# Decay attention with a softplus FFN on one core: operand moves on GpSimd's DMA queue, and a rearranged first batch

## The chip, the core and the metric

The kernel runs on one core of a Trainium2 chip. The metric is device time in microseconds (us); lower is better. A core has TensorE (PE in the profile, with its weight loads as PEld), VectorE (DVE), ScalarE (ACT), GpSimd (POOL) and SyncE (SP), which here only issues DMAs. Each engine has one instruction stream that it works through in order; the DMAs that an engine issues form its queue.

## What is computed

Two stages, in float32, one after the other on the same tokens. Batch 8, 8 heads, 576 positions, head size 64; the FFN has 512 inputs and outputs and 2048 hidden units.

```python
scores = scale * np.matmul(q, k.transpose(0, 1, 3, 2))       # scale = 1/8
cum = np.cumsum(np.log(np.clip(f, 0.0001, 1.0)), axis=-1)
decay = cum[:, :, :, None] - cum[:, :, None, :]
scores = np.where(causal, -1000000000.0, scores + decay)
attn = softmax(scores)                                       # over the last axis
x = (attn @ v), heads side by side: [4608, 512]
h = x @ w_in
g = np.maximum(h, 0.0) + np.log1p(np.exp(-np.abs(h)))
out = g @ w_out
```

The weights arrive as float64 and are turned into float32 on the chip (`load_f64`, line 422: a scaling and a sign part on ACT, a clip, a low part and a join).

## The kernel before

**The planner.** Nothing is emitted directly. Each piece of work is added to a list with a modelled cost on one engine (or on several to choose from), the pieces it comes after, and the buffers it takes (`Plan.add`, line 66). `Plan.run` (line 105) then simulates all engines and emits the piece that can start first, earlier-added pieces first among equals, until none is left. So modelled costs (`on_pe32`, `on_turn`, `on_dma`, from line 157) and due times set the order in which every engine's instructions stand in its stream. What the chip really takes shows only in the trace. Where the plan sees a gap on PE of over 0.5 us before the FFN's first accumulation, `fill_gap` (line 1487) puts small matmuls on a constant mask there (L1492), and three more such matmuls stand at the start (`warm`, L1481).

**The first batch ("plain").** Batch 0 is worked on in plain float32 matmuls, in 14 jobs: two quads (`first`, line 563: four heads, tokens 0 to 128), four pairs (`second`, line 573: two heads, tokens 128 to 256) and eight rests (`rest`, line 584: one head, tokens 256 to 576). The scores (L787) take q and k with two further rows, so that 66 rows are multiplied: the rows are the running sums `cum` and a constant of 8, in crossed order, and their products add the decay terms to the scores. They come by DMA: q and k from `in_qkT` (L687 for quads and pairs, L671 for rests), the two rows from the tile `cum` (L691, L674), each row by a DMA of its own. `cum` is made by a clip (L360), a logarithm (L363) and a scan in two steps: columns 0 to 256 (L376), then the rest (L381). Row minima (L794, on DVE), the exponential (L814, on ACT), transposes of the weights ("turn", L895), matmuls that spread the reciprocals (L899), and the product with v (L968, `output_tiled`) follow. In `output_tiled` the matmuls are grouped in one step for each bank of transposed weights. Meanwhile the weights are loaded (L440) in pieces of 512 KB; the FFN for tokens 0 to 256 is also plain (L1158 up, L1281 down).

**All other batches ("whole", line 552).** 56 jobs, one for each head of batches 1 to 7. Operands are split into a high and a low part, so that a product takes several faster matmuls. `prepare` (line 730) makes the tile `T` of a head: the high part of q and k by a cast (`hi`, L742), the low part by a subtraction (`lo`, L745), and four moves of 144 KB each from one half of the partitions to the other (L748), named k3, q1, k2 and q0 in the code. k3 comes after `hi`, q1 after `lo`, k2 after q1, and q0 after all of them, so that q1, k2 and q0 are three DMAs in a row. All four are issued by SP. The scores of the head (L789, L790) wait for q0. The weights of a head are scaled by the reciprocal sums before the turn (`scale`, line 839: on ACT L842, on DVE or POOL L844, as the plan chooses).

**Around them.** SP's queue also carries the loads of the next heads (L710 for q and k, L652 and L656 for v), the FFN's low weights (L1150, 512 KB each), its kept activations (L1236, L1317) and the output (L1359). The main loop (line 1496) adds, for each job in turn, its scores, turns and products, the `prepare` of the next job and the loads of the one after, some weight loads (`W_EACH`, line 1524: three for each job, two for each of the first six), and a share of the FFN's work that has come due.

Of the kernel before, what the change touches and what calls it, by code (L numbers as in the profile page):

```python
# [11 lines left out]
F32 = mybir.dt.float32  # L12
# [12 lines left out]
SCALE_BIAS = 1.0  # L25
# [25 lines left out]
class Plan:  # L51
# [53 lines left out]
    def run(self, engines):  # L105
        clock = dict.fromkeys(engines, 0.0)
        done, base, n = [False] * len(self.ops), 0, len(self.ops)
        while base < n:
            best = None
            for op in self.ops[base : base + WINDOW]:  # L110
                if done[op.at] or op.missing:
                    continue
                s = self.start_of(op, clock)
                if s and (best is None or (s[0], op.rank) < best[0]):
                    best = (s[0], op.rank), op, s
            _, op, (op.start, on) = best
# [42 lines left out]
    return On("PE", times * (max(n * 0.000444, m * 0.00092) + 0.002))  # L159


def on_pe32(n):

    return On("PE", 4 * n / 2400 + 0.004)


def on_turn(n):

    return On("PE", 0.109 * n)
# [49 lines left out]
def tile_decay_attention_softplus_ffn(  # L219
# [128 lines left out]


    decay_ready, cum_used, first_rows, cum = {}, [], [], {}  # L350

    def decay():
        box = {}
# [15 lines left out]
        def eights(e, t, value):  # L369
            e.memset(cum["x"][:, t, :], value)  # L370

        def scan(e):

            c = cum[0]
            x = box["f"][:, 0:256]
            e.tensor_tensor_scan(c[:, 0:256], x, x, 0.0, ALU.add, ALU.min)  # L376

        def scan_rest(e):
            c = cum[0]
            x = box["f"][:, 256:S]  # L380
            e.tensor_tensor_scan(c[:, 256:S], x, x, c[:, 255:256], ALU.add, ALU.min)  # L381

        def split(e):
            ch, cl = box["hl"] = [buf("raw", [P, S], f"c{x}", F32R)[0:BH] for x in "hl"]
# [37 lines left out]
    def load_f64(src, new, name, takes=()):  # L422
# [29 lines left out]
        def low(e):  # L452
            box["x"] = new()
            out = halves_of(box["x"], 2)[:, :, 0]
            x = halves_of(box["s"].rearrange("p c t -> p (c t)"), 4)[:, :, 1]
            scale, bias = 2.0**-13, 2.0**-14 - 0.5
            if e is nc.scalar:
                e.activation(out, x, AF.Copy, scale=scale, bias=bias)
            else:
                e.tensor_scalar(out, x, scale, bias, ALU.mult, ALU.add)  # L460

        def sign(e):
            out = halves_of(box["x"], 2)[:, :, 1].bitcast(F16)
# [8 lines left out]
        on = [On("POOL", 1.95), on_dve(512, True, bias=SCALE_BIAS)]  # L472
        cl = add(on, clip, after=[sc])
        lw = add(On("POOL", 1.95), low, after=[ld], takes=takes)
# [128 lines left out]
    def attention(job):  # L603
# [65 lines left out]
        def load32():  # L669
            def qk(e):  # L670
                e.dma_start(out=qk32[0:64], in_=qkT[b, :, heads[0]])  # L671

            def rows(e, x):
                e.dma_start(out=qk32[64 + x : 65 + x], in_=cum["x"][bh : bh + 1, 1 - x : 3 - x])  # L674
# [7 lines left out]
            cum_used.append(add(NO_ENGINE, mark, after=y))  # L682
            st["T"] = [x] + y

        def load_quad():
            def qk(e, h):
# [43 lines left out]
        def prepare():  # L730
# [26 lines left out]
            h_ = add(copies(S), hi, after=[start, st["qk"]])  # L757
            l_ = add(On("DVE", 0.75, 0.0, True), lo, after=[h_])
            give("raw", [l_])
            k3 = add_dma(move(low, 3, top, 0), 144, after=[h_])  # L760
            q1 = add_dma(move(low, 1, low, 2), 144, after=[l_])
            k2 = add_dma(move(low, 2, top, 0), 144, after=[q1])
            q0_ = add_dma(move(top, 0, low, 0), 144, after=[k2, k3, l_])
            st["T"] = [a, q0_]


        def stat_tile(ti):
# [12 lines left out]
            for i, (a, z, acc) in enumerate(pieces):  # L780
# [1 line left out]
                final = z == end  # L782

                def scores(e, box=box, a=a, z=z):
                    o = box["o"] = bank("att", f"s{n}_{ti}_{a}")[0:n_q, 0 : z - a]
                    if plain:
                        e.matmul(o, part32(0, q0, end), part32(1, a, z), start=True, stop=True)  # L787
                        return
                    e.matmul(o, qA[:, q0:end], kA[:, a:z], start=True, stop=False)  # L789
                    e.matmul(o, qB[0:ST, q0:end], kB[0:ST, a:z], start=False, stop=True)  # L790

                def row_min(e, box=box, w=z - a, i=i, final=final):
# [8 lines left out]
                o = add(on, scores, after=st["T"], takes=("att",), loose=True)  # L801
                m = add(
                    On("DVE", 0.076 + (z - a) / 960), row_min, lag=0.2, after=[o] + mask_set + stat_set,
                    takes=("stat",) if ti == 0 and i == 0 else (),
# [49 lines left out]
        def weights(bi):  # L854
# [69 lines left out]
            m = add(on_turn(len(blocks) - 0.48 * small + 2 * len(sums)), turn, after=need, takes=("att",))  # L924
# [18 lines left out]
        def output_tiled():  # L943

            steps = [[] for _ in banks]
            for gi, (g0, g1, r, c0) in enumerate(groups):
                todo = [x for x in parts if x[0] < g1 and x[1] > g0]
                todo.sort(key=lambda x: (max(x[0], g0) > g0, x[2]))
                for lo, hi, bi, vc, at, pbox, ready, _ in todo:
                    a, z = max(lo, g0), min(hi, g1)  # L950
                    mm = dict(
                        g=gi, r=64 * r, a=a - g0 + c0, z=z - g0 + c0, vc=vc, p=pbox, o=at + a - lo,
                        ready=ready,
                    )
                    steps[bi].append(mm)
                mms = [m for ms in steps for m in ms if m["g"] == gi]
                for m in mms:
                    m.update(start=m is mms[0], stop=m is mms[-1])
            box, before = {}, []
            for i, step in enumerate(steps):  # L960
                sides = [[m for m in step if m["r"] == r] for r in (0, 64)]
# [2 lines left out]
                def values(e, i=i, step=step):  # L964
# [8 lines left out]
                        )  # L973

                op = add(
                    on_pe32(max(sum(m["z"] - m["a"] for m in ms) for ms in sides)), values,
                    after=list(dict.fromkeys(x for m in step for x in m["ready"])) + before + st["V"],
                    takes=("att",) if i == 0 else (),
                )
                before = [op]  # L980
                used[i].append(op)

            puts = []
            for r, rows, c, w, bi, o, h, tok in job["puts"]:
# [109 lines left out]
    def ffn_block(i):  # L1094
# [48 lines left out]
        def up_part(u, k, half):  # L1143
# [41 lines left out]
            else:  # L1185
                need = st["load"]
            op = add(
                on_pe32(NCC * nt) if plain else on_pe(nt, 6), mm,
                after=st["split"] + need + st["ups"][-1:],
                takes=("h",) if first else (),  # L1190
            )
# [288 lines left out]
        for _ in range(WARM):  # L1480
            e.matmul(o[:, 0:MW], cmask[:, 0:P], cmask, start=True, stop=True)  # L1481

    give("h", [add(On("PE", 0.75 * WARM), warm, takes=("h",), after=mask_set)])

    filling = []

# [9 lines left out]
    for n in range(len(jobs) + 1):  # L1496
# [89 lines left out]
```

## Time and profile before

| | us |
|---|---|
| median of 3 runs | 1182.69 |
| the runs | 1180.13 to 1183.42 |
| the profiled execution, its time | 1187.69 |
| its span (first to last instruction) | 1185.9 |
| mean granted TensorE clock | 0.995 |
| ACT busy | 832.1 (70%) |
| DVE busy | 799.8 (67%) |

The profile is of one execution, on one core. The span lies within the execution's own time; the 1.79 us between them are before and after it. A row of the timeline gives the start, the length, the engine, the line, what is written from what, how often, and in brackets how long the engine had stood idle and what released it. An x after a group counts instructions. A plain float32 matmul stands as two of them. A row of the stages gives, for each stretch, the busy time (and count) of each engine, then the granted TensorE clock, the share of time that the 16 DMA engines were busy, and GB/s.

### The profile page before, as it was taken

To read this page: it belongs to the slowest core of one execution; us is meant where nothing else is said; L and a number is where in the kernel's file an instruction comes from. 1 tells how busy PE (TensorE), PEld (TensorE's weight loads), DVE (VectorE), ACT (ScalarE), POOL (GpSimd) and SP (SyncE) were. 2 spreads that over 40 slices of the span, in tenths; PEclk is the share of its full clock that TensorE was granted. 3 is DMA by queue.
4 is the path that set the end of the run, shared out by engine and by line. 5 is a ranking of instruction groups with operands and counts; after the bars stand their busy time and mean duration, and the time that the engine had idled before them with its cause. 6 is when DMAs were issued, how large, how long until landed. Compare 5 with 4: busy or idle time off the path is not lost.

```text
span 1185.9 us, 19896 instructions
## 1 busy us (share of the span) xinstructions
PE 1170.5 (99%) x6378; PEld 971.7 (82%) x6378; DVE 799.8 (67%) x1991; ACT 832.1 (70%) x1981; POOL 127.7 (11%) x139
## 2 busy tenths in 40 slices
PE   9999999999999999999999999999999999999998
PEld 7766779878888888888888888888888888888887
DVE  6877898877787678776776678667866773223322
ACT  5877787877886787677867777778767773444543
POOL 4211121110111011110000101001011010000000
PEclk9999999989999999999999999999999999999999
DMA  8856575555566555665566546656566433211210
GB/s 245 243 158 201 163 206 153 143 135 161 156 183 179 174 152 157 181 182 160 147 198 189 149 137 201 179 148 172 149 186 175 137 107 122 89 44 46 89 54 36
DMA packets 120776, 180.39 MB, mean 152 GB/s; under 512 B 22944, under 2 KB 80320, under 8 KB 120672
## 3 DMA queue, kind: packets, MB, share of 16 engines
q1 hardware_dynamic: 120648, 179.11, 52.5%
q8 instruction: 51, 0.84, 0.3%
q14 instruction: 53, 0.43, 0.1%
q10 hardware_dynamic: 24, 0.02, 0.0%
HBM read 109.98 MB, written 35.95 MB: 123 GB/s over the span
## 4 chain that ended last, share of the span: by engine, by line
PE 92%; DVE 4%; ACT 2%; DMA 1%; issue 1%; SPq 0%; POOL 0%; DVEq 0%; ACTq 0%; POOLq 0%
PE h L1177 31%; PE acc L1262 30%; PE b L895 8%; PE o L1027 7%; PE s L789 3%; PE s L790 3%; PE acc L1281 2%; PE h L1158 2%; PE s L787 2%; PE fill L1492 1%; PE o L968 1%; DMA T<-T 1%; ACT p L814 1%; DVE s L794 1%; DVE xl L1129 0%
## 5 line engine op out<-in xcount | busy, mean ns | idle before, releaser
L814 ACT ACTIVATE p<-s,negm 128x288 f32<-128x288 f32 (+7 forms) x384 | 183.3, 480 | 67.7 <-DVE negm L794 65.0
L1177 PE MATMUL h<-xh,wih 128*128 128x512 f32 (+1 forms) x576 | 229.9, 402 | 0.1
L1177 PE MATMUL h<-xl,wih 128*128 128x512 f32 (+1 forms) x576 | 217.7, 381 | 0.0
L794 DVE CUSTOM_DVE_ANT_0 s<-s,cmask 128x288 f32<-128x288 f32 (+6 forms) x320 | 138.0, 440 | 96.7 <-PE s L790 86.8
L1224 DVE SCALAR_TENSOR_TENSOR h<-h,e 128x512 f32<-128x512 f32 x136 | 95.8, 704 | 128.8 <-ACT e L1216 127.7
L844 POOL TENSOR_SCALAR p<-p,rsum 128x448 f32<-128x448 f32 (+4 forms) x85 | 95.1, 1127 | 763.6 <-DVE rsum L828 342.0
L1210 ACT ACTIVATE e<-h 128x512 f32<-128x512 f32 x144 | 86.0, 597 | 120.7 <-PE h L1177 116.5
L1262 PE MATMUL acc<-woh_dt_float32r,gh 128*128 128x512 f32 x376 | 153.1, 407 | 0.0
L1177 PE MATMUL h<-xh,wl 128*128 128x512 f32 (+1 forms) x576 | 149.0, 381 | 0.0
L1262 PE MATMUL acc<-woh_dt_float32r,gl 128*128 128x512 f32 x376 | 147.3, 392 | 0.1
L1262 PE MATMUL acc<-wol_dt_float32r,gh 128*128 128x512 f32 x376 | 146.9, 391 | 0.0
L921 DVE TENSOR_TENSOR pl<-b,ph 128x512 fp32r<-128x512 f32 x168 | 111.0, 666 | 21.0 <-ACT ph L215 17.8
L1177 PEld LDWEIGHTS h<-xh,wl 128*128 128x128 f32 x576 | 105.3, 189 | 21.5
L1177 PEld LDWEIGHTS h<-xh,wih 128*128 128x128 f32 x576 | 109.7, 190 | 15.7 <-PE b L895 0.3
L1177 PEld LDWEIGHTS h<-xl,wih 128*128 128x128 f32 x576 | 109.8, 191 | 14.8 <-DVE xl L1129 0.2
L1232 DVE TENSOR_TENSOR gl<-h,gh 128x512 fp32r<-128x512 f32 x136 | 93.6, 688 | 41.3 <-ACT gh L215 38.9
L895 PE MATMUL b<-ident,p 128*128 128x128 f32 (+1 forms) x728 | 118.5, 270 | 2.7 <-ACT p L215 1.7
L215 ACT CAST ph<-b 128x512 fp32r<-128x512 f32 (+2 forms) x167 | 82.1, 493 | 45.2 <-PE b L895 39.6
L215 ACT CAST gh<-h 128x512 fp32r<-128x512 f32 x113 | 66.4, 588 | 60.5 <-DVE h L1224 41.3
L895 PEld LDWEIGHTS b<-ident,p 128*128 128x128 f32 (+1 forms) x728 | 87.0, 139 | 19.3 <-issue 3.6
L789 PE MATMUL s<-T 128*64 128x64 f32 x336 | 97.6, 304 | 4.7 <-DMA T<-T 2.0
L790 PE MATMUL s<-T 68*64 68x64 f32 x336 | 98.0, 296 | 0.1
(153 smaller groups left out, 2224.0 us busy)
## 6 DMA issues: line engine op xcount, KB each, us to landing
wl<-wil_d SPq DMA_DIRECT2D x72, 512.0 KB
T<-T SPq DMA_DIRECT2D x224, 144.0 KB
raw<-in_qkT SPq DMA_DIRECT2D x112, 144.0 KB
g_d<-gh SPq DMA_DIRECT2D x84, 128.0 KB
g_d<-gl SPq DMA_DIRECT2D x84, 128.0 KB
vr<-in_vR SPq DMA_DIRECT2D x64, 160.0 KB
out<-ob SPq DMA_DIRECT2D x36, 256.0 KB
sto<-in_w_out SPq DMA_DIRECT2D x11, 512.0 KB
```

The source lines that it names most:

```text
L215: (e.tensor_copy if hasattr(e, "tensor_copy") else e.copy)(out, in_)
L789: e.matmul(o, qA[:, q0:end], kA[:, a:z], start=True, stop=False)
L790: e.matmul(o, qB[0:ST, q0:end], kB[0:ST, a:z], start=False, stop=True)
L794: e.tensor_tensor_reduce(out=box["o"], in0=box["o"], in1=cmask[0:n_q, right - w : right], scale=-0.125, scalar=m0 if i else 3.0e38, op0=AL ...
L814: e.activation(o, box["o"], AF.Exp, bias=m1, scale=-1.0, accum_out=acc)
L844: e.tensor_scalar(a, a, f_, None, ALU.mult)
L895: e.transpose(box["ps"][0 : x.shape[1], at : at + one.shape[1]], x, one)
L921: e.tensor_sub(box["l"], box["ps"][:, 0:w], box["h"].bitcast(F32))
L1177: e.matmul(o, l, r, start=m == 0, stop=m == 11)
L1224: e.scalar_tensor_tensor(h, h, 0.0, box["e"], ALU.max, ALU.add)
L1232: e.tensor_sub(box["l"], box["t"], box["h"].bitcast(F32))
L1262: e.matmul(st["acc", tt], l, r[fc], start=first and m == 0, stop=last and m == 2,)
```

## The change

- In `prepare`, the four moves k3, q1, k2 and q0 are issued by POOL instead of SP. Their dependences stay.
- The quads' scores are multiplied over 64 rows and wait only for q and k. The two decay terms are added into the same bank by two further float32 matmuls (`sums`): the running sums times 8 on the diagonal of a 64x64 tile, and the tile with -8 times the running sums. The two tiles (`eye8`) are made at the start. The DMAs of the two rows stay, for the pairs.
- The scan is in three steps, to 128, 256 and 576 columns.
- The scores of every plain tile are now 128 columns wide on PE, where the first tile of a rest was 64 wide; the other half of the output isn't read.
- The two rows of a rest come by one DMA instead of two.
- The product with v of a rest is one step instead of three, and its banks are given back together.
- For each of the first six jobs one piece of weights is loaded instead of two.
- The clip of the weights goes to DVE only; modelled costs change (low part on POOL 0.85 us instead of 1.95, 0.19 us more for a step of `output_tiled` and about that for a turn with sums, 5% more for plain up parts, 1.3 instead of 0.75 us for a warm matmul).
- No fill is put ahead of PE's first instruction.

```diff
-                elif op.start - clock["PE"] > 0.5:
+                elif clock["PE"] and op.start - clock["PE"] > 0.5:
...
+    eye8 = [cpool.tile([BH, BH], F32, name=f"eye8{x}") for x in "pm"]
...
-        decay_ready["first"] = add(On("DVE", 0.63), scan, after=[l])
-        c = decay_ready["sums"] = add(On("DVE", 0.78), scan_rest, after=[decay_ready["first"]])
+        c = l
+        for x, a, z in (("quad", 0, P), ("first", P, 2 * P), ("sums", 2 * P, S)):
+            on = On("DVE", 0.11 + (z - a) / 480)
+            c = decay_ready[x] = add(on, lambda e, a=a, z=z: scan(e, a, z), after=[c])
...
-                return heads32(heads[a // P], 1)[0:ST0, 0, which, 0:P]
+                return heads32(heads[a // P], 1)[0:64, 0, which, 0:P]
...
-            y = [
-                add_dma(lambda e, r=r: rows(e, r), 4, after=[start, decay_ready["sums"]] + first_rows)
-                for r in range(2)
-            ]
+            y = add_dma(rows, 9, after=[start, decay_ready["sums"]] + first_rows)
...
-            st["T"] = T_of[heads[0]] = T_of[heads[2]] = x + y
+            st["T"] = x
+            T_of[heads[0]] = T_of[heads[2]] = x + y
...
-            k3 = add_dma(move(low, 3, top, 0), 144, after=[h_])
-            q1 = add_dma(move(low, 1, low, 2), 144, after=[l_])
-            k2 = add_dma(move(low, 2, top, 0), 144, after=[q1])
-            q0_ = add_dma(move(top, 0, low, 0), 144, after=[k2, k3, l_])
+            k3 = add_dma(move(low, 3, top, 0), 144, eng="POOL", after=[h_])
+            q1 = add_dma(move(low, 1, low, 2), 144, eng="POOL", after=[l_])
+            k2 = add_dma(move(low, 2, top, 0), 144, eng="POOL", after=[q1])
+            q0_ = add_dma(move(top, 0, low, 0), 144, eng="POOL", after=[k2, k3, l_])
...
-                        e.matmul(o, part32(0, q0, end), part32(1, a, z), start=True, stop=True)
+                        e.matmul(
+                            o, part32(0, q0, q0 + P), part32(1, a, z), start=True, stop=not quad,
+                        )
...
+                def sums(e, box=box, h=heads[ti % len(heads)]):
+                    c, (plus, minus) = cum[0][:, 0:P], (x[:, h : h + 1].to_broadcast([BH, P]) for x in eye8)
+                    e.matmul(box["o"], c, plus, start=False, stop=False)
+                    e.matmul(box["o"], minus, c, start=False, stop=True)
...
+                if quad:
+                    o = add(on_pe32(2 * P), sums, after=[o, decay_ready["quad"]] + eye8_set)
...
+            if not quad and not pair:
+                steps = [sum(steps, [])]
...
-            for _ in range(W_EACH if n >= nfirst else W_EACH - 1):
+            for _ in range(W_EACH if n >= nfirst else 1):
```

More of the change, by code (lines that the diff above doesn't have):

```diff
@@ L159, in on_pe, with on_pe32 @@
     return On("PE", times * (max(n * 0.000444, m * 0.00092) + 0.002))
-def on_pe32(n):
-    return On("PE", 4 * n / 2400 + 0.004)
+def on_pe32(n, switch=False):
+    return On("PE", 4 * n / 2400 + 0.004 + 0.19 * switch)
 def on_turn(n):
@@ L350, in tile_decay_attention_softplus_ffn @@
     decay_ready, cum_used, first_rows, cum = {}, [], [], {}
+    eye8 = [cpool.tile([BH, BH], F32, name=f"eye8{x}") for x in "pm"]
+    eye8_set = [
+        add(
+            [on_act(BH), on_dve(BH, True)],
+            lambda e, x=x, v=v: e.mul(x, ident[0:BH, 0:BH], v) if e is nc.scalar
+            else e.tensor_scalar(x, ident[0:BH, 0:BH], v, None, ALU.mult),
+        )
+        for x, v in zip(eye8, (8.0, -8.0))
+    ]
     def decay():
@@ L370, in eights, with scan @@
             e.memset(cum["x"][:, t, :], value)
[L372 to L381, printed above, removed]
+        def scan(e, a, z):
+            c, x = cum[0], box["f"][:, a:z]
+            e.tensor_tensor_scan(c[:, a:z], x, x, c[:, a - 1 : a] if a else 0.0, ALU.add, ALU.min)
         def split(e):
@@ L455, in low @@
             x = halves_of(box["s"].rearrange("p c t -> p (c t)"), 4)[:, :, 1]
[L456 to L460, printed above, removed]
+            e.tensor_scalar(out, x, 2.0**-13, 2.0**-14 - 0.5, ALU.mult, ALU.add)
         def sign(e):
@@ L471, in load_f64 @@
         sc = add(on_act(512, 0.04), scale, after=[ld], takes=("fe",))
-        on = [On("POOL", 1.95), on_dve(512, True, bias=SCALE_BIAS)]
-        cl = add(on, clip, after=[sc])
-        lw = add(On("POOL", 1.95), low, after=[ld], takes=takes)
+        cl = add(on_dve(512, True), clip, after=[sc])
+        lw = add(On("POOL", 0.85, 0.0, True), low, after=[ld], takes=takes)
         give(stag, [sc, lw])
@@ L671, in qk, with rows @@
                 e.dma_start(out=qk32[0:64], in_=qkT[b, :, heads[0]])
-            def rows(e, x):
-                e.dma_start(out=qk32[64 + x : 65 + x], in_=cum["x"][bh : bh + 1, 1 - x : 3 - x])
+            def rows(e):
+                x = cum["x"][bh : bh + 1, 0:2]
+                planes = bass.AP(x.tensor, x.offset, [x.ap[0], [S, 2], [S, 2], [1, S]])
+                e.dma_start(out=qk32[64:ST0], in_=planes)
             start = add(NO_ENGINE, mark, takes=("T0",), lag=0.0)
             x = add_dma(qk, 288, after=[start] + first_rows)
-            y = [
-                add_dma(lambda e, r=r: rows(e, r), 4, after=[start, decay_ready["sums"]] + first_rows)
-                for r in range(2)
-            ]
-            cum_used.append(add(NO_ENGINE, mark, after=y))
-            st["T"] = [x] + y
+            y = add_dma(rows, 9, after=[start, decay_ready["sums"]] + first_rows)
+            cum_used.append(add(NO_ENGINE, mark, after=[y]))
+            st["T"] = [x, y]
         def load_quad():
@@ L784, in scores @@
                 def scores(e, box=box, a=a, z=z):
-                    o = box["o"] = bank("att", f"s{n}_{ti}_{a}")[0:n_q, 0 : z - a]
+                    o = bank("att", f"s{n}_{ti}_{a}")[:, 0 : z - a]
+                    box["o"] = o[0:n_q]
                     if plain:
-                        e.matmul(o, part32(0, q0, end), part32(1, a, z), start=True, stop=True)
+                        e.matmul(
+                            o, part32(0, q0, q0 + P), part32(1, a, z), start=True, stop=not quad,
+                        )
                         return
+                    o = box["o"]
                     e.matmul(o, qA[:, q0:end], kA[:, a:z], start=True, stop=False)
@@ L923, in weights @@
             need = list(dict.fromkeys(need)) + halves_set
-            m = add(on_turn(len(blocks) - 0.48 * small + 2 * len(sums)), turn, after=need, takes=("att",))
+            m = add(on_turn(len(blocks) - 0.48 * small + 2 * len(sums) + 1.7 * bool(sums)), turn, after=need, takes=("att",))
             st.setdefault("turned", []).append(m)
@@ L975, in output_tiled @@
                 op = add(
-                    on_pe32(max(sum(m["z"] - m["a"] for m in ms) for ms in sides)), values,
+                    on_pe32(max(sum(m["z"] - m["a"] for m in ms) for ms in sides), True), values,
                     after=list(dict.fromkeys(x for m in step for x in m["ready"])) + before + st["V"],
@@ L980, in output_tiled @@
                 before = [op]
-                used[i].append(op)
+                for bi in range(len(banks)) if len(steps) == 1 else (i,):
+                    used[bi].append(op)
             puts = []
@@ L1187, in up_part @@
             op = add(
-                on_pe32(NCC * nt) if plain else on_pe(nt, 6), mm,
+                on_pe32(1.05 * NCC * nt) if plain else on_pe(nt, 6), mm,
                 after=st["split"] + need + st["ups"][-1:],
@@ L1481, in warm @@
             e.matmul(o[:, 0:MW], cmask[:, 0:P], cmask, start=True, stop=True)
-    give("h", [add(On("PE", 0.75 * WARM), warm, takes=("h",), after=mask_set)])
+    give("h", [add(On("PE", 1.3 * WARM), warm, takes=("h",), after=mask_set)])
     filling = []
```

1 line of the change is left out of this document (added).

## The prediction

> **What bounds the kernel now.** I read the page first, then the stages, then the timelines of single engines where PE is not full.
>
> ```profile
> span 1185.9 us, 19896 instructions
> PE 1170.5 (99%) x6378; PEld 971.7 (82%) x6378; DVE 799.8 (67%) x1991; ACT 832.1 (70%) x1981; POOL 127.7 (11%) x139
> ```
>
> PE is the bound: only 15.4 us of the span are idle on it. An edit can therefore only pay through PE's idle time, through work that PE does for nothing, or through its clock. The stages say where these lie (the first row has all engines, PE, PEld, DVE, ACT and POOL; the next three PE alone; the last the fills of L1492 alone; then come the granted clock, the DMA share and GB/s):
>
> ```profile
> 10.18:60.00 49.82, 48.39 (x366) 36.11 (x365) 42.98 (x129) 41.26 (x103) 18.04 (x20) 1.00 0.83 259
> ...
> 60.00:160.00 100.00, 98.48 (x661) 1.00 0.64 180
> 160.00:260.00 100.00, 94.59 (x579) 0.95 0.56 152
> 260.00:1000.00 740.00, 738.11 (x3937) 1.00 0.58 164
> ...
> 10.18:60.00 49.82, 11.57 (x84) 9.92 (x82) 1.00 0.83 259
> ```
>
> Up to 10.18 us PE does no real work, as the timeline below shows. From there to 60 us it is idle for 1.43 us, and 11.57 us of its busy time are fills: 13.0 us to be had. From 60 to 160 us 1.5 us are idle. From 160 to 260 us, where the first whole heads run, 5.4 us are idle and the clock stands at 0.95, which is another 5 us. In the 740 us after that only 1.9 us are idle. So the change can gain in the first 60 us and from 160 to 260 us; in the long middle it can only lose.
>
> **The quads' start.** PE, DVE and SP in the first microseconds:
>
> ```profile
> 1.39 2.07 PE L1492 MATMUL fill<-cmask 128*128 128x128 f32 x8 [1.39 <-POOL cmask L314]
> 3.26 4.19 PE L1481 MATMUL warm<-cmask 128*128 128x448 f32 x6
> 7.28 3.06 PE L1492 MATMUL fill<-cmask 128*128 128x128 f32 x26
> 10.18 1.06 PE L787 MATMUL s<-T 66*128 66x128 f32 x8
> ...
> 1.36 1.33 SPq L687 DMA_DIRECT2D T<-in_qkT  x2
> 5.38 1.62 SPq L691 DMA_DIRECT2D T<-cum  x2
> ...
> 4.66 0.68 DVE L376 TENSOR_TENSOR_SCAN cum<-fs 64x256 f32<-64x256 f32 x1 [0.75 <-ACT fs L363]
> 10.73 0.30 DVE L794 CUSTOM_DVE_ANT_0 s<-s,cmask 128x128 f32<-128x128 f32 x1 [4.17 <-PE s L787]
> ```
>
> The q and k of the first quad are issued by 2.69 us, but its scores start at 10.18 us, 4.8 us after the two row DMAs begin to be issued behind the scan. The change takes the rows out of this wait. What is late next? First q and k themselves, for which I have two rows:
>
> ```profile
> 2.00:4.00 2.00, 2.00 (x8) 1.60 (x8) 0.60 (x1) 0.05 (x2) 1.61 (x8) 1.00 0.66 187
> 4.00:6.00 2.00, 2.00 (x4) 1.01 (x3) 1.30 (x2) 0.63 (x1) 0.00 (x0) 1.00 1.11 222
> ```
>
> 187 and 222 GB/s bring 0.37 MB by 4 us, and the 0.66 MB of `f` (64x576 floats) and of two loads of 256 KB (64 rows of four times 256 floats) by about 5.3 us; with half a microsecond for the landing, 5.9 us. Second the warm matmuls, which lose the fill ahead of them (1.87 us from start to start, work for nothing) and so end near 7.28 - 1.87 = 5.4 us. Third the new matmuls, which need the first half of the 0.68 us scan, so cum at 5.1 us, and two tiles of 64x64 that ACT and DVE can make in their idle time. I take 6.1 us for the first scores. The four score matmuls at 10.18 take 1.06 us, 0.265 each, so a tile with its two sums is ready 0.8 us later and the first row minimum starts near 7.1 us (with 0.2 until DVE takes it) instead of 10.73: **3.6 us gained**. The bounds are 0, if the loads of v that SP issues in between hold q and k back, and 4.1. The 16 new matmuls are 16 x 0.265 = 4.2 us on PE, which I cost at nothing as they lie among fills; if this cover is gone, it is 4.2 us lost. The pairs still wait for the rows, which have landed by 10.18 us as the row above shows.
>
> **The rests' loads, the weights' pace.** The longest fill, and the first load for a rest:
>
> ```profile
> 36.29 3.39 PE L1492 MATMUL fill<-cmask 128*128 128x128 f32 x28
> ...
> 27.64 0.54 SPq L671 DMA_DIRECT2D T<-in_qkT  x1
> ```
>
> PE has the longest time without work just as the rests begin. Ahead of the load at 27.64 us SP's queue holds weights, and with one piece for a job instead of two the rests come forward. How much of the 13.0 us then goes is set by what is full beside PE: in the row of 10.18 us DVE is busy for 42.98 of 49.82 us, ACT for 41.26, the DMA engines for 0.83 of the time. If DVE reaches 95%, its work takes 45.2 us: **4.6 us gained**. Bounds: 0, if the postponed weights leave the plain FFN waiting instead, and 11, if the postponed weight work frees DVE as well. One DMA for the two rows of a rest takes eight issues off SP, for which nobody waits: nothing. The clip's place and the removed ACT form: nothing, the plan can choose as it did.
>
> **Less switching on PE.** A rest's first tile is 64 wide. Rows that show it beside others:
>
> ```profile
> 95.22 0.75 PE L787 MATMUL s<-T 66*64 66x320 f32 x2
> 95.90 1.12 PE L1281 MATMUL acc<-wol_dt_float,g 128*128 128x512 f32 x2
> ...
> 97.84 0.92 PE L787 MATMUL s<-T 66*128 66x448 f32 x2
> 98.60 1.95 PE L1158 MATMUL h<-x,woh_dt_float 128*128 128x128 f32 x16
> ```
>
> A 128 wide tile of 448 columns takes 0.76 us from start to start, so one of 320 would take 0.54; the 64 wide one takes 0.68. That is 0.14 us for each of eight rests; I count five of them, as the first few lie among fills: **0.7 us gained**. The bounds are 0 and 2.2, if the switch into the narrow tile costs as much as the one out of it. The one step for the product with v can save such switches only where other work stands between the steps now; I cost it at nothing, with the same 0.14 us for each of 16 joints, 2.2 us, as its other bound.
>
> **The moves on POOL's queue.** In the steady part a head's q0 is long there when the scores start, and one DMA of the 224 costs SP half a microsecond:
>
> ```profile
> 554.20 0.54 SPq L748 DMA_DIRECT2D T<-T  x1
> 567.22 0.19 PE L789 MATMUL s<-T 128*64 128x64 f32 x1
> ...
> L748 SPq DMA_DIRECT2D T<-T x224: 461/489/720, 111.5 to 954.3; - x112
> ```
>
> 13.0 us lie between the last move and its scores. Moves that are slower by some microseconds change nothing there; I cost that part at nothing. It is different in the stage from 160 us, with the heads one after another. The moves of one such head, SP's rows around them, and PE:
>
> ```profile
> 162.58 2.41 SPq L748 DMA_DIRECT2D T<-T  x2
> ...
> 167.29 0.54 SPq L1359 DMA_DIRECT2D out<-ob  x1
> 169.25 0.48 SPq L748 DMA_DIRECT2D T<-T  x1
> 171.56 0.59 SPq L1150 DMA_DIRECT2D wl<-wil_d  x1
> 172.26 0.48 SPq L748 DMA_DIRECT2D T<-T  x1
> ...
> 176.87 0.21 PE L789 MATMUL s<-T 128*64 128x64 f32 x1 [1.60 <-DMA T<-T]
> ...
> 175.00:180.00 5.00, 3.35 (x19) 0.75 0.70 202
> 180.00:185.00 5.00, 5.00 (x35) 0.91 0.49 117
> ```
>
> k3 and q1 are issued by 165.0, k2 at 169.25 behind an output, q0 at 172.26 behind 512 KB of weights; the scores follow at 176.87. From q1 to landing the three moves in a row take 11.9 us, 4.0 each. PE idles 1.60 us, and the clock then stands at 0.75 and 0.91 for 5 us each, which is 1.7 us more: 3.3 us in all. On POOL the moves stand behind nothing but POOL's own scalings, so k2 goes out as soon as q1 has landed. No POOL DMA is in the trace. Bounds for one move by the nearest rows: 3.0 us, within which k2 had landed here (169.25 to 172.26), and 6 us, one and a half times the loaded 4.0. I take a value between 3.0 and 4.0, as these rows are SP's with other work ahead, and count half of the stall as gone, since the order of this stage will change and other stalls can come: **1.6 us gained** (0 to 3.3; the loss is a rival below). Behind a waiting move on POOL stand the scalings of L844, and behind these the turns on PE; the plan can give these scalings to ACT or DVE, and POOL is 11% busy. Nothing.
>
> The Trainium skill, "DMA: Bandwidth & Descriptors", section "Issuing engines are not separate DMA queues", speaks against a gain: all issuing engines use the same 16 DMA engines, and another one saves only the time to start a DMA. By that, this term would be nothing, and the time 1174. The trace has the moves behind other issues, which that sentence does not cover.
>
> On the clock, the skill's "TensorE: Matmul & The Clock Gate", Part 1, drops it after an idle window of about 3.4 us; by that the 1.60 us stall would cost 1.6 and not 3.3. The row of 175 us differs, and the measurement decides.
>
> **The sum.** -3.6 - 4.6 - 0.7 - 1.6 = -10.5 us. The profiled execution took 1187.69 us (span 1185.9 and 1.79 around it), which gives 1177.2; it stands 5.0 us above the median of the runs, 1182.69, so the same change makes 1172.2 of the median, and I forecast 1172. A measurement of this kernel can tell about 0.3%, 3.5 us, from no change.
>
> **Rivals.**
>
> *Late moves (slower).* POOL's way could be slower than SP's loaded one. DVE and POOL hinder each other in this trace: the same cast takes 0.97 us while POOL works (first row), and 0.42 at another time.
>
> ```profile
> 21.62 2.23 POOL L460 TENSOR_SCALAR wol_dt_float<-sto 128x512 uint16<-128x512 uint16 x2 [0.45 <-DMA sto<-in_w_out]
> 23.16 0.97 DVE L215 CAST wih<-woh_dt_float 128x512 fp32r<-128x512 f32 x1
> 32.61 0.42 DVE L215 CAST wih<-woh_dt_float 128x512 fp32r<-128x512 f32 x1
> ...
> 163.77 0.21 PE L789 MATMUL s<-T 128*64 128x64 f32 x1 [0.60 <-PE o L1027]
> ```
>
> If a move takes 6 us, the three in a row take 18 instead of 11.9. Between 160 and 260 us some eight heads run, by the 13.1 us that lie between two of them (176.87 and the row below). I estimate that five have no slack; each is then late by about 4 us and brings 1.7 us of lower clock: 28 us lost, 8.9 gained elsewhere, 1202. It decides from the point where a move takes about 4.6 us: five heads that are 1.8 us late eat the 8.9. Against it: the free queue, and 13 us of slack later. Chance 0.16. A rule of the Trainium skill points the same way ("SBUF — State Buffer", section "SBUF: two separate sides"): while DVE runs a two-port operation, GpSimd can't write the descriptors of its DMAs. By it a move would wait for the end of such an operation, and no run so far shows one.
>
> *The start is spent waiting for weights (no change).* The plain FFN starts when its fourth piece of weights is joined, and a slower pace of weights does not hurry that:
>
> ```profile
> 27.59 0.67 DVE L468 SCALAR_TENSOR_TENSOR woh_dt_float<-ti,woh_dt_float 128x512 uint32<-128x512 uint32 x1
> 27.98 2.84 PE L1158 MATMUL h<-x,woh_dt_float 128*128 128x128 f32 x24
> ```
>
> Then PE fills 3.6 us more before 28 us, the rests wait for DVE, and the moves gain nothing; only 0.7 us is left, 1182. Chance 0.10.
>
> *All of it goes.* 4.1, 11, 2.2, and in the stage from 160 us all 5.4 us of idle time and the 5 of the clock: 27.7 us, 1155. Chance 0.06.
>
> **The numbers.** The forecast has 0.68. Its terms alone reach from 1164 (with 11 instead of 4.6 and the stall wholly gone) to 1178 (without cover for the sums, and no gain from the moves). For 8 in 10 I go from 1160, toward the third rival, to 1184, past the second. Faster by over 0.3%: forecast and third rival, 0.74. Within it: the second, 0.10. Slower: the first, 0.16.
>
> **What would show it.** Right: the first row minimum near 7 us; fills from 10 to 60 us at 7 us or less; rests' first tiles at 0.54 us from start to start; the stage from 160 to 260 us (shifted by 10) with less than 4.5 us idle and a clock over 0.95; less than 3 us idle in the 740 after it. Wrong: scores that wait for T in more than two places, DVE operations or POOL's scalings lengthened in the steady part, fills that have only moved toward 28 us.

## The result, and the profile after

The change made the kernel slower: 1189.92 us median of 13 runs (1184.96 to 1201.46), beside 1182.62 us for 13 runs of the kernel before on the same chip; ratio 1.0072 (1.0045 to 1.0099). The forecast was 1172, and its range ended at 1184.

The profiled execution took 1193.04 us. The head of its page, and its groups for the moves:

```profile
span 1191.3 us, 19644 instructions
PE 1164.2 (98%) x6300; PEld 964.3 (81%) x6300; DVE 796.0 (67%) x1982; ACT 850.3 (71%) x2040; POOL 204.5 (17%) x316
...
L747 POOL DMA_DIRECT2D T<-T x224 | 119.6, 534 | 673.2 <-ACT T L215 312.0
```

PE is busy for 6.3 us less than before and idle for 27.1 us where it was 15.4. The 224 moves now stand on POOL, 0.53 us for starting one. The same stages as in the prediction, PE alone:

```profile
10.18:60.00 49.82, 48.34 (x309) 0.86 0.76 234
60.00:160.00 100.00, 94.99 (x655) 1.00 0.72 204
160.00:260.00 100.00, 93.32 (x583) 1.00 0.54 147
260.00:1000.00 740.00, 732.39 (x3899) 1.00 0.58 163
```

Idle time grew in every stage from 60 us on: 5.0 us (1.5 before), 6.7 (5.4), and 7.6 in the long middle (1.9), which the prediction had costed at nothing. The first stage has lost 14% of its clock. PE's waits name the cause of most of the idle time (total, times, longest):

```profile
PE s L792 <- DMA T<-T: 13.9, 9, 3.0
PE warm L1495 <- POOL cmask L335: 2.1, 1, 2.1
PE b L906 <- ACT p L825: 2.0, 2, 1.0
```

Before, scores waited for the moves (`T<-T`) twice, 2.0 us in all. Now it is nine times: four between 137 and 222 us (7.8 us), and five in the middle, 6.1 us, one for every eighth head. Here is the first of these five, POOL's rows of the timeline and then PE's:

```profile
340.01 0.52 POOL L747 DMA_DIRECT2D T<-T  x1 [5.51 <-ACT T L215]
341.97 0.52 POOL L747 DMA_DIRECT2D T<-T  x1 [1.45 <-DVE T L744]
342.60 2.15 POOL L855 TENSOR_SCALAR p<-p,rsum 64x64 f32<-64x64 f32 x2
345.77 0.57 POOL L747 DMA_DIRECT2D T<-T  x1 [1.03 <-DMA T<-T]
350.90 1.16 POOL L747 DMA_DIRECT2D T<-T  x2 [4.56 <-PE s L793]
...
354.60 0.21 PE L792 MATMUL s<-T 128*64 128x64 f32 x1 [1.48 <-DMA T<-T]
```

q1 starts at 341.97, as soon as the low part is written, k2 at 345.77, q0 at 350.90. From q1's start to the scores it takes 12.6 us for three moves, and the scores come as soon as q0 lands. Nothing blocks the moves for long; PE is simply there before them. (The first of the two starts at 350.90 is q0; the second is the next head's k3.)

The quads' start went nearly as forecast. PE and DVE:

```profile
6.50 0.48 PE L787 MATMUL s<-T 64*128 64x128 f32 x2
6.83 0.38 PE L805 MATMUL s<-eye8p,cum 64*128 64x128 f32 x2
7.05 0.38 PE L806 MATMUL s<-cum,eye8m 64*128 64x128 f32 x2
7.27 0.38 PE L787 MATMUL s<-T 64*128 64x128 f32 x2
...
9.37 0.94 PE L1506 MATMUL fill<-cmask 128*128 128x128 f32 x6
...
18.55 0.33 PE L906 MATMUL b<-ident,p 128*128 128x128 f32 x1 [1.04 <-ACT p L825]
...
7.59 0.30 DVE L797 CUSTOM_DVE_ANT_0 s<-s,cmask 128x128 f32<-128x128 f32 x1 [0.73 <-PE s L806]
```

The first row minimum starts at 7.59 us (forecast 7.1, 10.73 before), and fills are down from 16.5 us to 0.9. The profile's clock record shows half rate from 19.7 to 33.4 us, 1.2 us after the idle time ahead of 18.55 us: 6.8 us lost.

### The profile page after: what moved, and what is told of

It reads as the page before. It is cut to its first block, busy times and chain, and to the rows that moved or that the text cites. A ratio compares the mean times of both kernels' runs of the same rounds, so it can differ in the third digit from the quotient of the medians.

```text
span 1191.3 us, 19644 instructions
## 1 busy us (share of the span) xinstructions
PE 1164.2 (98%) x6300; PEld 964.3 (81%) x6300; DVE 796.0 (67%) x1982; ACT 850.3 (71%) x2040; POOL 204.5 (17%) x316
## 3 DMA queue, kind: packets, MB, share of 16 engines
q0 software_dynamic: 10752, 33.04, 11.1%
## 4 chain that ended last, share of the span: by engine, by line
PE 71%; DMA 7%; DVE 6%; ACT 5%; issue 2%; DVEq 0%; SPq 0%; POOLq 0%; ACTq 0%
PE h L1191 28%; PE acc L1276 26%; DMA T<-T 6%; PE b L906 6%; PE o L1041 5%; PE s L793 3%; PE s L792 3%; DVE s L797 1%; ACT p L825 1%; DVE h L1238 1%; DVE gl L1246 1%; ACT e L1230 1%; ACT e L1227 1%; ACT p L853 1%; DVE pl L932 1%
## 5 line engine op out<-in xcount | busy, mean ns | idle before, releaser
L747 POOL DMA_DIRECT2D T<-T x224 | 119.6, 534 | 673.2 <-ACT T L215 312.0
L215 ACT CAST ph<-b 128x512 fp32r<-128x512 f32 (+2 forms) x183 | 89.2, 490 | 58.1 <-PE b L906 52.8
L792 PE MATMUL s<-T 128*64 128x64 f32 x336 | 99.4, 304 | 14.5 <-DMA T<-T 13.9
L853 ACT ACTIVATE p<-p,rsum 128x192 f32<-128x192 f32 (+4 forms) x225 | 105.8, 535 | 3.8 <-DVE rsum L839 3.5
```

Source lines behind the costliest of these rows:

```text
L747: return lambda e: e.dma_start(out=tb[to, i, :], in_=tb[of, j, :])
L853: e.activation(a, a, AF.Copy, scale=f_)
```

## The experiments

My theory at the outset had two parts. One: the planner models a move on POOL's queue with 2.65 us, 7.9 us for three. In the trace three moves on POOL take about 10.6 us on average over the 740 us (from q1's start to q0's landing); on SP's queue in the kernel before they took about 10.3. So POOL's way would not be slower to speak of; the order of PE's stream, made from the low price, would bring the scores too early. Two: without fills the clock falls near 20 us. The first rival: POOL's queue itself is the slower way, whatever the plan. The second: the moves matter little, and the start makes the time.

All times are medians of 4 to 12 runs, ratios against the kernel before on the same chip; its medians there were 1182.6 to 1183.1 us. The waits are of the one profiled execution.

| kernel | us | fastest run | ratio (95% interval) | waits for T, us |
|---|---|---|---|---|
| e1, after with moves on SP | 1168.8 | 1167.1 | 0.9902 (0.9866 to 0.9938) | none shown |
| e2, before with moves on POOL | 1194.2 | 1188.4 | 1.0098 (1.0072 to 1.0125) | 10.1 |
| e3, after, price +0.9 | 1184.7 | 1181.1 | 1.0023 (1.0006 to 1.0040) | 8.0 |
| e4, after's plan, SP's queue | 1185.2 | 1181.0 | 1.0020 (1.0002 to 1.0038) | 1.9 |
| e5, after, price +1.8 | 1178.0 | 1175.4 | 0.9979 (0.9947 to 1.0010) | none shown |
| e6, e5 with cheaper starts | 1181.3 | 1179.1 | 0.9995 (0.9981 to 1.0010) | none shown |
| e7, e1 with the old pace of weights | 1177.1 | 1175.4 | 0.9963 (0.9941 to 0.9986) | 1.0 |
| e8, e1 with the old quads | 1178.2 | 1168.8 | 0.9950 (0.9924 to 0.9976) | 0.6 |
| e9, after with fills | 1193.3 | 1192.5 | 1.0096 (1.0083 to 1.0109) | 15.2 |
| e10, after, price +1.3 | 1184.5 | 1179.2 | 1.0024 (1.0007 to 1.0041) | 3.6 |
| e11, e1 with values in several steps | 1174.9 | 1172.4 | 0.9935 (0.9923 to 0.9947) | 0.9 |
| e12, e1's plan, POOL's queue | 1182.9 | 1177.7 | 1.0010 (0.9985 to 1.0035) | 6.5 |

**e1, the moves back on SP.** Plan and queue.

```diff
-            k3 = add_dma(move(low, 3, top, 0), 144, eng="POOL", after=[h_])
+            k3 = add_dma(move(low, 3, top, 0), 144, after=[h_])
```

q1, k2 and q0 alike.

> The kernel after, with the four moves within SBUF of each head back on SyncE's queue, in the plan and on the chip; start, quads, sums and weights stay changed. Theory (moves on GpSimd's queue make a head's scores wait for T; kernel after: 9 waits, 13.9 us): the scores' wait for T falls to 4 us or less, PE's idle time from 27 to about 16 us, and the time to 1176 to 1181 us, below the kernel before (1182.6) because the start's gain stays. Rival (the start without fills, whose clock drop costs 6.8 us, is what makes it slow): the time stays at 1186 to 1190 us, and half clock shows between 15 and 40 us.

Measured: 1168.8, better than the theory expected, and the best kernel of the case: 14 us below before, 21 below after. Its stages, PE alone:

```profile
10.18:60.00 49.82, 48.92 (x323) 0.90 0.78 243
60.00:160.00 100.00, 97.43 (x667) 1.00 0.73 202
160.00:260.00 100.00, 97.97 (x620) 1.00 0.59 162
260.00:1000.00 740.00, 738.72 (x3931) 1.00 0.57 163
```

Beside after's rows, 13.4 us of idle time are gone between 60 and 1000 us (19.3 to 5.9 us). This execution too had half rate near 22 us (0.90), so that part is not what parts the two. The second rival falls.

**e2, the moves alone.** The same edit the other way, on the kernel before.

> The kernel before, with only the four moves of each head on GpSimd's queue, in the plan and on the chip; its start with the fills is untouched. Theory: the scores' wait for T grows from 2.0 us to 8 to 14 us, and the time from 1182.6 to 1187 to 1195 us. Rival (the start is the cause): within 3 us of the kernel before.

```profile
PE s L789 <- DMA T<-T: 10.1, 9, 2.9
```

Measured: 11.4 us slower. The moves on POOL cost time without the rest of the change too, and there are nine waits again, five of them at every eighth head.

**e3, an honest price.** In the planner's model of a DMA's landing:

```diff
-    return each * (n - 1) + 2.1 + kb / n / RATE - on_dma(kb, n, eng).cost
+    late = 0.9 if eng == "POOL" else 0.0
+    return each * (n - 1) + 2.1 + late + kb / n / RATE - on_dma(kb, n, eng).cost
```

> The kernel after, moves still on GpSimd's queue, but the planner counts 0.9 us more for each of them, so that its chain of a head's moves (10.6 us) is the measured one. Theory (the planner's price is too low, so that PE's stream has the scores too early): the scores' wait for T falls from 13.9 to 4 us or less and the time to 1178 to 1183 us. Rival (GpSimd's queue itself is too slow or too uneven for the slack there is): waits of 8 us or more stay, and the time is within 3 us of the kernel after (1189.9).

```profile
PE s L793 <- DMA T<-T: 8.0, 7, 2.0
```

A miss on both: 8.0 us of waits stay, as the rival had it, and the time came down by 5 us only, above the 1178 to 1183 of the theory. In the plan of after, by its modelled times, every eighth head had some 3 us between q0's landing and its scores. With 0.9 us more for a move the plan did not put these scores later; it only used up that margin (0.8 us left), so at these heads PE's order stayed. A mean price is not enough for moves that take 2.2 to 6.0 us.

**e4, after's order with SP's queue.** The plan untouched:

```diff
-                return lambda e: e.dma_start(out=tb[to, i, :], in_=tb[of, j, :])
+                return lambda e: nc.sync.dma_start(out=tb[to, i, :], in_=tb[of, j, :])
```

> The kernel after with its plan (every engine's order) unchanged, but the moves issued by SyncE. Theory (it is the plan's price, and the two chains last about the same: 10.3 us by SyncE, 10.6 by GpSimd): waits for T of 8 us or more remain and the time is within 4 us of the kernel after. Rival (GpSimd's queue itself is the slower way): the waits for T fall to 4 us or less and the time to 1178 to 1181 us.

```profile
PE s L792 <- DMA vr<-in_vR: 2.6, 1, 2.6
PE s L792 <- DMA T<-T: 1.9, 2, 1.0
PE h L1191 <- DVE gl L1246: 1.7, 2, 1.3
```

A second miss for the theory as it stood: by SP the same order leaves 1.9 us of waits for T, as the rival had it. So POOL's queue is slower where it counts: over the 740 us three moves take about 9.6 us here and 10.6 in after. The time, 1185.2, lies between theory and rival, 16 us above that of e1, which has the same queue. So this order is worse in other ways too; the waits name a load of v, which now stands behind moves that the plan did not expect on SP, and what the rest is stays open.

**e12, e1's order with POOL's queue.** The counterpart, with the same edit (`nc.gpsimd`) on e1.

> The counterpart of the kernel with GpSimd's plan and SyncE's queue: the plan of the kernel with the moves on SyncE (1168.8 us) unchanged, but the moves are issued by GpSimd. Theory (it is the order that the plan makes from the price, not the queue): the scores' wait for T stays at 4 us or less and the time is 1169 to 1175 us. Rival (GpSimd's queue itself costs what was lost: its moves now also stand behind the 84 scalings of GpSimd): waits of 8 us or more, and 1180 us or more.

The waits, 6.5 us, lie between theory and rival; the time is the rival's, 14 us above e1, and a miss for the theory. The profiled execution is the slowest of twelve, with loads at 188 GB/s from 10 to 60 us (243 in e1), so its waits are read with care; the fastest of the twelve is still 10.6 us above e1's fastest. With after, e1 and e4 these are four kernels that differ in the order and the queue of the moves alone (medians, and the fastest runs in brackets):

| | SP's queue | POOL's queue |
|---|---|---|
| order of e1 | 1168.8 (1167.1) | 1182.9 (1177.7) |
| order of after | 1185.2 (1181.0) | 1189.9 (1185.0) |

POOL's queue costs time in either order, 14 us and 5. The order that was drawn up with POOL's modelled price costs time on either queue, 16 us and 7: it is the worse one even on the queue that it was made for.

**e5, e10, room in the plan.** As e3, with 1.8 and with 1.3 us.

> The kernel after, moves on GpSimd's queue, but the planner counts 1.8 us more for each, 13.3 us for a head's chain of moves where 10.6 were measured: unlike with 0.9 us more, the plan now has to put scores later. Theory (on GpSimd's queue a chain lasts about 10.6 us, and the stream of PE only has to leave it room): the scores' wait for T falls from 13.9 us to 3 us or less, and the time from 1189.9 to 1176 to 1182 us, not down to the 1168.8 of the kernel with the moves on SyncE, since the plan itself is 5 us longer. Rival (GpSimd's moves are uneven, with a tail that no reasonable price covers): 6 us or more of these waits stay, and the time is above 1183 us.

```profile
10.18:60.00 49.82, 48.53 (x356) 1.00 0.78 252
60.00:160.00 100.00, 96.30 (x652) 1.00 0.72 199
160.00:260.00 100.00, 93.65 (x568) 0.97 0.54 146
260.00:1000.00 740.00, 738.99 (x3933) 1.00 0.58 164
```

As expected: no waits for T are listed any more (one of 2.5 us is left, see below), the middle is down to 1.0 us idle, and the time falls by 12 us with the same queue and nothing but a number changed in the model. The 9 us that remain to e1 lie mostly between 160 and 260 us (6.4 us idle, clock 0.97). There the three moves take 11.2 us on average (9.6 in after), and three times 1.9 to 3.8 us pass between k2's landing and q0's start, where 0.7 is usual: in the higher price's order, k3 of the next head stands ahead of q0, and waits for its cast. POOL and then PE in that stage:

```profile
227.43 1.14 POOL L748 DMA_DIRECT2D T<-T  x2 [4.94 <-ACT T L216]
...
230.46 0.21 PE L793 MATMUL s<-T 128*64 128x64 f32 x1 [2.47 <-issue]
```

The second of the two moves at 227.43 is q0. For the idle time in front of the scores the profile names no releaser, but q0, which starts at 228.05, takes 2.3 us to land, and the scores start 0.1 us later: this too is a wait for the moves.

> The kernel after, moves on GpSimd's queue, with 1.3 us more in the planner's price of a move (chain 11.8 us; 13.3 gave 1178.0 us, 10.6 gave 1184.7). Theory (the price has only to cover the measured 10.6 us and its spread; what is counted beyond that is lost): waits for T of 4 us or less, and 1174 to 1178 us. Rival (the whole 1.8 us are needed): 4 to 8 us of the waits are back, and 1179 us or more.

A miss on the time: 1184.5, although only 3.6 us of waits are back. The waits do fall with the price: 13.9 us without any, 8.0 with 0.9, 3.6 with 1.3, 2.5 with 1.8. But every change of a price draws up the whole order anew, and a few microseconds come with it either way.

**e6, cheaper starts.** e5 with 0.55 us of POOL's time for starting a move in the model, in place of 1.5.

> The kernel before this one, and the planner also counts 0.55 us of GpSimd's time for starting a move (measured: 0.53) in place of 1.5, so that GpSimd gets back scalings that went to ScalarE (84 before, 38 after). Theory (ScalarE's additional work is the second part of the loss between 60 and 260 us): ScalarE's busy time falls from 849 to about 835 us and the time is 3 to 8 us below that of the kernel before this one. Rival (ScalarE's work is not what PE waits for): within 2 us of it, or longer, if scalings now stand ahead of moves.

```profile
PE b L907 <- ACT p L826: 5.3, 7, 2.2
```

POOL got its scalings back (85) and ACT's busy time fell to 833.6 us, as expected, but the time did not: 1181.3. So nothing here shows the work that the change pushed onto ACT to be what was lost.

**e7, e8, e11, the other parts.** One part of the change undone in e1 each time.

```diff
-            for _ in range(W_EACH if n >= nfirst else 1):
+            for _ in range(W_EACH if n >= nfirst else W_EACH - 1):
```

> The kernel with the four moves on SyncE (1168.8 us), with the old pace of weights: two pieces for a job in the first jobs in place of one. The prediction's term for the rests' loads and the weights' pace is 4.6 us (bounds 0 and 11): 1173 us, and fills or waits of 4 us or more back between 20 and 60 us. Rival (the gain there is that of the quads' start and the plan, not of the pace): within 2 us of 1168.8.

e8 also has the 66 rows of before in its scores, and no sums:

```diff
-            st["T"] = x
-            T_of[heads[0]] = T_of[heads[2]] = x + y
+            st["T"] = T_of[heads[0]] = T_of[heads[2]] = x + y
```

> The kernel with the four moves on SyncE (1168.8 us), with the quads' scores over 66 rows again, waiting for the two row loads, without the 16 matmuls of the sums. The prediction's term for the quads' start is 3.6 us (bounds 0 and 4.1) with the sums costed at nothing: 1172 us, first row minimum near 10.7 us instead of 7.6. Rival (the sums' 3.5 us on PE eat most of the start's gain, since no fills cover them any more): within 1.5 us of 1168.8.

```diff
-            if not quad and not pair:
-                steps = [sum(steps, [])]
```

> The kernel with the four moves on SyncE (1168.8 us), with the product with v of a rest in its several steps again. The prediction cost the one step at nothing, with 2.2 us as its other bound: 1168 to 1171 us. Rival (the plan gains more by it, since PE's stream has fewer joints to wait at): 1172 us or more.

The pace of the weights is worth 8.4 us (8.3 by the fastest runs), more than the 4.6 expected, and 5.0 us of fills are back between 20 and 60 us. The one step is worth 6.2 (5.3), as the rival had it. The quads' start is worth little: e8's twelve runs fall into two groups, five at 1168.8 to 1170.6 with clocks of 0.998 and more, and seven at 1177.6 to 1184.3 with 0.986 to 0.991. The first group lies 1.5 us or so above e1's four fastest (1167.1 to 1168.8), though its first row minimum comes 3.2 us later than e1's (8.41 us):

```profile
11.64 0.30 DVE L796 CUSTOM_DVE_ANT_0 s<-s,cmask 128x128 f32<-128x128 f32 x1 [4.84 <-PE s L786]
```

Whether the old start brings half rate on more often, six runs of e1 are too few to tell.

**e9, fills in the start.**

```diff
+                elif clock["PE"] and op.start < 24 and op.start - clock["PE"] > 0.1:
+                    self.fill(engines["PE"], 0.65)
```

> The kernel after with two fills (128x128 matmuls for nothing, 0.22 us each) at each of the planner's gaps over 0.14 us between 8 and 24 us on TensorE, six places. Theory (the kernel after loses some 5 us in most runs to half clock near 20 us, which follows an idle time of about 1 us that the fills of the kernel before would have covered): no half clock between 15 and 40 us, the runs' mean clock at 0.998 or more, and the time 3 to 5 us below the kernel after (1189.9), since the fills themselves cost 1 to 2 us; the scores' wait for T stays at 10 to 16 us. Rival (the clock falls for reasons of its own): the mean clock stays at 0.995 and the time is within 2 us of the kernel after.

The kernel had three fills at each of the six places, not two, 4 us in all. Its stage from 10.18 to 60 us kept its clock:

```profile
10.18:60.00 49.82, 49.78 (x373) 1.00 0.79 250
```

But the runs' mean clock stayed at 0.995 to 0.998, since half rate came elsewhere (3.4 us from 219.9 us in the profiled execution), and the time rose. The theory's second part falls as an explanation of the result: the fall of the clock at the start costs its 5 to 7 us in an execution that has it, but fills against it cost as much. After's two runs at a clock of 1.000 took 1185.0 and 1185.4 us, and e9's best, at 0.998, 1192.5. Those two are also above the fastest run of before, 1179.65, so after is slower at full clock too.

## Why the prediction was wrong

**The step that failed** is "Moves that are slower by some microseconds change nothing there; I cost that part at nothing." The 13.0 us between q0 and its scores were true for the head that I had looked at. Heads are not alike. That head had 10.7 us from q0's landing to its scores; by the landings in the trace of before, one head in eight had between 0.1 and 3.1 us in the same stretch. And these margins were not kept: the order is drawn up from modelled prices, and the change priced a move at 2.65 us on a queue that the model takes to be free, where SP's had been modelled with the work in it. So the scores moved up just where the moves became slower: at these five heads 12.6 to 14.2 us pass from q1's start to the scores in the trace of before, 11.2 to 11.4 in e4, which has after's order and no wait for T there, and 13.8 in e5. In after the moves themselves took 11.9 to 12.5. It took both, the order and the queue: in the 740 us PE is idle for 1.3 us in e1, 1.1 with after's order alone (e4), 2.7 with POOL's queue alone (e12), and 7.6 in after. After minus e1 is +21 us for the term that I had put at -1.6. Of these, 12 go with a price that leaves room (after to e5), and 9 stay on POOL's queue even then (e5 to e1). That the price is the cause of the 12 is shown by e5, and that the order and the queue each cost time by the four kernels beside e12; the split itself is rough, as e10 shows.

**The size of a move** was right: I took 3 to 4 us, and the median from start to landing is 3.1 us on POOL. But I put it into a picture of the old order. Of the two rules that I had weighed, the Trainium skill's "DMA: Bandwidth & Descriptors", section "Issuing engines are not separate DMA queues", gave nothing for this term; in e4 and after the same order takes about 9.6 and 10.6 us for three moves, so the issuing engine did matter here, and the other way than for a gain. The Trainium skill's "SBUF — State Buffer", section "SBUF: two separate sides", by which a move would wait for DVE, does not show in the starts: one on POOL took 518 ns in the median, which is also the shortest, and 1042 at the longest. Whether it is in the 3.1 us to the landing, the trace does not tell.

**The late-moves rival** had the right mechanism in part, late scores but not the new order, and the wrong point. It was to decide from 4.6 us for a move, and in the five tightest heads of one stage alone, "13 us of slack later" speaking against it. It decided at 3.1 us for a move (the median), or 3.5 (a third of the three moves' 10.6), and five of the nine waits lie in the stretch that I had excluded. Its sum also had heads 4 us late for three moves made 6.1 us longer, and gave no reason for the difference. The wait in more than two places, named under what would show the forecast wrong, is what the profile showed.

**The other terms** came to -8.9 us; e1 has -14.0 (1168.8 beside 1182.8). By parts:

- *Quads' start, -3.6:* its mechanism was right (7.59 us, forecast 7.1), its worth was not. The 16 matmuls of the sums take 0.22 us each, 3.5 us on PE, and were costed at nothing "as they lie among fills". e8 shows about 1.5 us at full clock for start and sums together. That the sums take what the start gains, since the fills were gone, is argued: no run has the new start without them.
- *Loads and weights, -4.6 (0 to 11):* right in sign and place, mis-sized: 8.4.
- *Switching, -0.7:* a rest's first tile of 320 columns now takes 0.54 us from start to start, as forecast:

```profile
99.79 0.70 PE L787 MATMUL s<-T 66*128 66x320 f32 x2
100.33 1.02 PE L1295 MATMUL acc<-wol_dt_float,g 128*128 128x512 f32 x2
```

- *One step for v, nothing, with 2.2 as its other bound:* 6.2, outside the bound. I had counted switches on PE; that the joints also let the plan put other work between, and so order DVE and PE differently, I had not. That reading is argued, not shown.

**Fills as pure gain.** I counted 11.57 us of fills as time to be had. They also keep PE from standing idle. After's runs spread over 16.5 us (spans from 1183.2 us at a mean clock of 1.000 to 1199.7 at 0.989), those of before over 7.1; that this comes from the missing fills is not shown. What brings half rate on in one execution and not in the next stays open.

## What to carry to other kernels

In a kernel whose order comes from modelled costs, moving work to another queue changes two things, the queue and the price, and the price may reorder everything: compare the model's number for the new queue with a measured one, and leave room for the spread, before counting anything as free. Read slack from the tightest of the recurring places, not from one that happens to be quoted. And a part that fails can hide good ones: here the other parts gave 14 us once the moves were taken out.

## What the runs showed of the hardware

A 144 KB move within SBUF took a median of 3.1 us from start to landing on POOL's queue (2.2 to 6.0), and 2.4 by SP in the kernel before; over the 740 us the means are closer, 3.2 and 3.0. On POOL a move also starts no sooner than 0.39 us (k2) and 0.66 us (q0) after the landing that it waits for; in e4, by SP, the shortest is 0.02 us, with 0.3 and 0.5 on average. So the way by POOL, which starts a move in 0.53 us, is still the slower one. The page of after lists these moves as `q0 software_dynamic`, 10752 packets for 33.04 MB, where all of SP's stand under `q1 hardware_dynamic`; whether that is the reason is not shown. Half rate comes in steps of 3.4 us (3.4, 6.8, 10.2 and 13.7 us long). It followed idle times of 1.04 us (after) and 0.87 us (e1) near 20 us, but not the idle time of 2.97 us in this row of after, whose stages have a clock of 1.00:

```profile
161.00 0.21 PE L792 MATMUL s<-T 128*64 128x64 f32 x1 [2.97 <-DMA T<-T]
```

So the length of one idle time does not decide it.
